# Linear attention's first chunk on Trainium2: reciprocals spread by quarter-array products, folded weights by halves, diagonal blocks set by GpSimd copies

## The chip, the cores and the metric

The kernel runs on one core of one Trainium2 chip, in one launch. The metric is the device time in microseconds; the profiled execution gives every instruction's start and duration. Five engines run side by side, each working through its own queue in order and waiting on semaphores: TensorE (PE; its weight loads are shown as PEld), VectorE (DVE), ScalarE (ACT), GpSimd (POOL) and SyncE (SP), which here issues the DMA transfers.

## The reference

Four layers act on x of 2048 rows by 576 columns in bf16: attention, MLP, attention, MLP, each added to x. The kernel calls them layers 0 to 3; the change touches layers 0 and 2.

```python
def _A_ref(x, wqkv, wo):                       # H = 32 heads of Dh = 18
    q, k, v = ...(x @ wqkv)...
    phi = lambda t: jnp.where(t > 0, t + 1, jnp.exp(t)) + 1e-6
    pq, pk = phi(q), phi(k)
    kv = jnp.einsum("bhsd,bhse->bhde", pk, v)
    z = jnp.einsum("bhsd->bhd", pk)
    num = jnp.einsum("bhqd,bhde->bhqe", pq, kv)
    den = jnp.einsum("bhqd,bhd->bhq", pq, z)[..., None] + 1e-6
    o = num / den
    return ...(o)... @ wo
def _B_ref(x, w1, b1, w2, b2):
    y = _layernorm(x, axis=-1)
    return gelu(y @ w1 + b1) @ w2 + b2
x = x + _A_ref(_layernorm(x), A_wqkv, A_wo)
x = x + _B_ref(_layernorm(x), B_w1, B_b1, B_w2, B_b2)   # and both once more
```

## The kernel before

The 2048 rows are 16 row blocks (t) of 128, in four chunks (c) of 512. The 32 heads are five groups (g): four of 7 heads (126 columns) and one of 4 heads (72 columns). The queries are held with their columns on the partitions, so a query tile pq[(g, c)] has 126 (or 72) partitions and 512 rows of x along it.

An attention layer (layer_A) first makes keys and query tiles for most of x. Its second part, where the change lies, runs once the sum over all keys is there:

- z (L789) and from it zsel, which sums a head's columns against z.
- den_stage(c), L820 to L828: 20 small TensorE products give the denominators of a chunk, 32 heads by 4 row blocks on 128 partitions; ScalarE takes the logarithm (L824) and the exponential of its negative (L827), which leaves the reciprocals in the single tile rden.
- quad_stage(c), L834: VectorE multiplies rden with a mask of four diagonal blocks, quad_mask, into a 128x512 tile quad_rden.
- scale_stage(g, c): one 512-wide TensorE product with head_bc (L847) spreads the reciprocals of a group over its 18 columns a head; ScalarE copies the bank (L851), VectorE multiplies the query tile (L852). With direct=True VectorE reads the bank itself.
- quarter_stage(c), L863, for later chunks: 16 products of 32 rows by 126 columns, 128 wide, for groups 0 to 3; each uses a quarter of TensorE's rows, takes rden as it is and needs no diagonal blocks. ScalarE copies four banks into the scratch tile turned (L867); quarter_scale multiplies (L873). Group 4 of these chunks still goes through scale_stage, and so through quad_rden.
- kv_groups (L693, then L699 and L704 with a mask) gives kvT; kv_wo(g) and kv_wo_half(g, half) fold the output weights into it: two 288-wide products a group, copied to kvwo. Groups 0 and 1 are folded earlier by halves (L711, L716), groups 2 to 4 here by kv_wo through a pair of banks (L799), copied by ScalarE (L806) or VectorE (L804).
- wo_stage(t), L883: ten products a row block, then the residual sum on VectorE (L598), the store of x, and for the first four row blocks the LayerNorm of the next layer. For these GpSimd takes the power (L428), one small product (L431), the normalised rows (L461) and a copy of their last 64 columns (L469).

TensorE's order is written out by hand: every product is chained to the one before (pe), so a product that waits holds everything behind it. The order of the other queues comes from a scheduler, steered by manual dependencies such as dve_after or "sums first".

PSUM has four single banks (ps_h, used in turn; a new use waits until the last reader is done) and two pairs, accA and accB (ps_acc). TensorE's order in the edited part is: a query product, den_stage(0), kv_groups, the second query product, folding of groups 2 and 3, three spreading products, folding of group 4, the fourth, the third query product, the fifth, den_stage(1), the last query product, row block 0. The four query products there (q_left) belong to chunk 3. In the loop over t, den_stage(2) and (3) come at t = 2 and t = 5, quarter_stage(1), (2), (3) at t = 1, 3, 7, and scale_stage(4, c) at t = 2, 4, 8.

Of the kernel before, what the change touches and what calls it, by code (L numbers as in the profile page):

```python
# [8 lines left out]
ALU = mybir.AluOpType  # L9
# [6 lines left out]
P = 128  # L16
# [18 lines left out]
def build(tc, A_x, A_wqkv, A_wo, B_w1, B_b1, B_w2, B_b2, out, dbg=None, n_layers=4):  # L35
    nc = tc.nc
    dbg = dbg or {}
    with ExitStack() as ctx:
# [23 lines left out]
        quad_mask = const.tile([P, 4, P], BF16, name="quad_mask")  # L62
# [15 lines left out]
        def cut(start, shape, fill, op, base, pattern, mult):  # L78
# [15 lines left out]
            cut(8, (4,), 0.0, ALU.is_ge, 0, [[-32, 4]], 1),  # L94
            cut(8, (4,), 0.0, ALU.is_ge, 31, [[32, 4]], -1),
# [163 lines left out]
        dve_last = dict(norm=None, sum=None, phi=None)  # L259
# [280 lines left out]
        def phi_from_psum(ps_ap, out_ap, rows, n, turned_cols=False, after=None, dve_after=None, exp_first=False,  # L540
                          tag=None):
# [11 lines left out]
            low = nc.vector.tensor_scalar(out=e[0:rows, 0:n], in0=e[0:rows, 0:n], scalar1=1.0, scalar2=1e-6,  # L553
                                          op0=ALU.min, op1=ALU.add)
            top = nc.vector.tensor_tensor(out=out_ap, in0=a[0:rows, 0:n], in1=e[0:rows, 0:n], op=ALU.max)
            if dve_after is not None:
                tc.add_manual_dep(top.ins, dve_after, NOSYNC, reason="denominators first")
            dve_last["phi"] = top.ins.name
            if tag is not None:
                named("e" + tag, exp), named("id" + tag, ident_pass), named("mi" + tag, low), named("ma" + tag, top)  # L560
# [47 lines left out]
        def layer_A(li, next_kind, pre_a1=None):  # L608
            pq = {}

            def q_proj(g, c, defer=False):
# [5 lines left out]
                pq[(g, c)] = first_pq if first_pq is not None and (g, c) == (0, 0) else \  # L617
                        blk.tile([P, D], BF16, name="pq", tag="blk")
                if g == 0:
                    if first_pq is None or c > 0:  # L620
                        (nc.gpsimd if li > 0 else nc.vector).memset(pq[(g, c)][96:P, 0:CA], 1.0)
# [64 lines left out]
            def kv_groups(groups):  # L686
# [12 lines left out]
                nc.vector.tensor_tensor(  # L699
# [3 lines left out]
                if 4 in groups:  # L703
                    nc.vector.tensor_tensor(  # L704
                        out=kvT[0:72, 4, 0:72].rearrange("p (h e) -> p h e", h=4),
                        in0=ps[0:72, 126 * n:126 * n + 72].rearrange("p (h e) -> p h e", h=4),
                        in1=maskz[0:72, 0:4, :], op=ALU.mult)
# [88 lines left out]
            def kv_wo(g):  # L796
                wp = ps_acc.tile([P, 2, 512], F32, name="kvwo_ps", tag=("accB", "accA")[g % 2])
                for half in range(2):
                    pe(nc.tensor.matmul(wp[0:GR[g], half, 0:HALF], lhsT=kvT[0:GR[g], g, 0:GR[g]],  # L799
                                     rhs=wo_sb[0:GR[g], g, half * HALF:(half + 1) * HALF], start=True, stop=True))  # L800
                kvwo[g] = blk.tile([P, D], BF16, name="kvwo", tag="blk")
                out = kvwo[g][0:GR[g], :].rearrange("p (h n) -> p h n", h=2)
                if g in (3, 4):
                    nc.vector.tensor_copy(out=out, in_=wp[0:GR[g], :, 0:HALF])  # L804
                else:
                    act_last["kvwo"] = nc.scalar.copy(out=out, in_=wp[0:GR[g], :, 0:HALF]).ins.name  # L806

            quad_rden = {}
            rden_of = {}
            rden_now = {}  # L810

            def den_stage(c, after=None, pair=None):
# [16 lines left out]
                rden_of[c] = rden  # L829
                rden_now["tile"] = rden  # L830

            def quad_stage(c, after=None):
                quad = blk.tile([P, D], BF16, name="quad_rden", tag="blk")
                spread_out = nc.vector.tensor_tensor(  # L834
                    out=quad[:, 0:CA].rearrange("p (j n) -> p j n", j=4), in0=quad_mask[:],
                    in1=rden_of.pop(c)[:].unsqueeze(1).to_broadcast([P, 4, P]), op=ALU.mult)
                if after is not None:
                    tc.add_manual_dep(spread_out.ins, after, NOSYNC, reason="sums first")
                quad_rden[c] = quad
                dve_last["quad"] = spread_out.ins.name  # L840

            def scale_stage(g, c, pair=None, direct=False):
# [4 lines left out]
                pe(nc.tensor.matmul(bp[:, 0:CA], lhsT=head_bc[:, g, :], rhs=quad_rden[c][:, 0:CA], start=True, stop=True))  # L847
                spread_rows = bp
                if not direct:
                    spread_rows = blk.tile([P, D], BF16, name="rden_bc", tag="blk")  # L850
                    act_last["copy"] = nc.scalar.copy(out=spread_rows[0:GR[g], 0:CA], in_=bp[0:GR[g], :]).ins.name  # L851
                mult = nc.vector.tensor_tensor(out=pq[(g, c)][0:GR[g], 0:CA], in0=pq[(g, c)][0:GR[g], 0:CA],  # L852
                                               in1=spread_rows[0:GR[g], 0:CA], op=ALU.mult)
                dve_last["mult"] = mult.ins.name

            def quarter_stage(c):

                rden = rden_now["tile"]
                banks = [ps_h.tile([P, 512], F32, name="rden_ps", tag="h") for _ in range(4)]
# [6 lines left out]
                for i in range(4):  # L866
                    act_last["copy"] = nc.scalar.copy(out=spread_rows[0:126, i, 0:4 * P], in_=banks[i][0:126, :]).ins.name  # L867

            def quarter_scale(c, groups, after):
                spread_rows = turned[:].rearrange("p a t c -> p (a t c)").rearrange("p (i w) -> p i w", i=4)  # L870
                for g in groups:
# [4 lines left out]
                    dve_last["mult"] = mult.ins.name  # L876
# [292 lines left out]
```

## Time and profile before

| | us |
|---|---|
| median of 3 runs (762.48 to 763.7) | 762.74 |
| profiled execution | 762.86 |
| its span in the profile | 761.1 |
| TensorE busy | 755.4 (99%) |
| ScalarE busy | 327.4 (43%) |
| VectorE busy | 271.2 (36%) |
| GpSimd busy | 119.1 (16%) |

The profiled execution is 1.76 us longer than its span. The granted TensorE clock is full in all slices. Layer 0's edited part runs from 70 to 104 us, layer 2's from 442 to 476 us.

In the timeline a row is: start, duration, engine, line, operation, output<-input, sizes and count, and in brackets the idle time ahead of it on its engine and what ended it. Rows with a count cover instructions that follow each other; TensorE's products are pipelined, so a product's row is longer than the time until the next one starts, and starts are what to compare.

### The profile page before, as it was taken

To read this page: it belongs to the slowest core of one execution; us is meant where nothing else is said; L and a number is where in the kernel's file an instruction comes from. 1 tells how busy PE (TensorE), PEld (TensorE's weight loads), DVE (VectorE), ACT (ScalarE), POOL (GpSimd) and SP (SyncE) were. 2 spreads that over 40 slices of the span, in tenths; PEclk is the share of its full clock that TensorE was granted. 3 is DMA by queue.
4 is the path that set the end of the run, shared out by engine and by line. 5 is a ranking of instruction groups with operands and counts; after the bars stand their busy time and mean duration, and the time that the engine had idled before them with its cause. 6 is when DMAs were issued, how large, how long until landed. Compare 5 with 4: busy or idle time off the path is not lost.

```text
span 761.1 us, 15693 instructions
## 1 busy us (share of the span) xinstructions
PE 755.4 (99%) x6539; PEld 489.0 (64%) x6539; DVE 271.2 (36%) x683; ACT 327.4 (43%) x731; POOL 119.1 (16%) x194
## 2 busy tenths in 40 slices
PE   8999999999999999999999999999999999999998
PEld 5777654774477457646777767447645754674476
DVE  8875962136023503401455678600230132000000
ACT  6884756205600650263056566560164036205600
POOL 4840341002000301200100005300020020001000
PEclk9999999999999999999999999999999999999999
DMA  8992573017302711320246007530240033011000
GB/s 255 267 309 51 169 269 83 16 58 196 82 31 84 185 53 47 108 69 16 73 122 202 1 32 244 193 83 16 76 104 29 16 125 83 9 32 55 2 10 23
DMA packets 80897, 73.82 MB, mean 97 GB/s; under 512 B 36730, under 2 KB 65466, under 8 KB 80826
## 3 DMA queue, kind: packets, MB, share of 16 engines
q1 hardware_dynamic: 80826, 72.82, 32.9%
q8 instruction: 51, 0.84, 0.5%
q14 instruction: 20, 0.16, 0.1%
HBM read 48.03 MB, written 24.77 MB: 96 GB/s over the span
## 4 chain that ended last, share of the span: by engine, by line
PE 94%; DMA 2%; DVE 2%; ACT 1%; issue 0%; SPq 0%; DVEq 0%; ACTq 0%
PE m_ps L1060 36%; PE h_ps L1002 20%; PE hp_ps L1002 16%; PE q_ps L614 6%; PE k_ps L644 5%; PE k_ps L669 4%; PE wo_ps L883 2%; PE m_half L1060 1%; PE k_tail L669 1%; DMA xo<-x_d 1%; DMA x_d<-xo 1%; PE tp L493 1%; ACT turned L867 1%; DMA x<-in_A_x_dram 0%; PE kv_ps L693 0%
## 5 line engine op out<-in xcount | busy, mean ns | idle before, releaser
L1060 PE MATMUL m_ps<-w_sb,hT 128*128 128x288 bf16 x2232 | 274.8, 286 | 0.0
L1060 PEld LDWEIGHTS <-hT 128*128 128x128 bf16 x2304 | 224.8, 98 | 59.8 <-issue 3.4
L1002 PEld LDWEIGHTS <-w_sb 64*128 64x128 bf16 x2304 | 124.5, 94 | 136.5 <-issue 1.9
L1002 PE MATMUL hp_ps<-yT,w_sb 64*128 64x512 bf16 x1152 | 178.0, 376 | 0.0
L1002 PE MATMUL h_ps<-yT,w_sb 64*128 64x512 bf16 x1152 | 148.0, 376 | 0.0
L1007 ACT COPY relay_sb<-relay_sb 128x1 f32<-128x1 f32 x144 | 28.6, 198 | 260.2 <-PE h_ps L1002 217.9
L998 ACT ACTIVATE hT<-h_ps,b1T 128x512 bf16<-128x512 f32 x144 | 91.2, 684 | 44.4 <-PE h_ps L1002 44.4
L428 POOL TENSOR_TENSOR ln_rstd<-ln_u,neg_half 128x1 f32<-128x1 f32 x61 | 35.4, 581 | 408.3 <-DVE ln_u L410 225.3
L998 ACT ACTIVATE hT<-hp_ps,b1T 128x512 bf16<-128x512 f32 x144 | 91.2, 693 | 0.0
L598 DVE TENSOR_TENSOR xbf<-m_ps,xo 128x576 bf16<-128x576 f32 x15 | 11.4, 758 | 212.9 <-PE m_ps L1060 212.9
L598 DVE TENSOR_TENSOR xo<-m_ps,xo 128x576 f32<-128x576 f32 x16 | 12.1, 757 | 176.5 <-PE m_ps L1060 176.5
L581 POOL TENSOR_TENSOR xo<-xo,b_bc 128x576 f32<-128x576 f32 x32 | 40.9, 1284 | 101.3 <-DMA xo<-x_d 62.7
L1002 PE MATMUL h_ps<-yT,w_tail 64*128 64x512 bf16 x144 | 54.1, 376 | 0.0
L1002 PE MATMUL hp_ps<-yT,w_tail 64*128 64x512 bf16 x144 | 54.1, 376 | 0.0
L614 PE MATMUL q_ps<-yT,wqkv_sb 128*126 128x512 bf16 (+1 forms) x200 | 49.5, 379 | 0.0
L644 PE MATMUL k_ps<-wqkv_sb,yT 128*128 128x288 bf16 x320 | 47.0, 286 | 0.3 <-ACT yT L495 0.3
L883 PE MATMUL wo_ps<-kvwo,pq 126*128 126x288 bf16 (+1 forms) x320 | 44.5, 286 | 0.2
L1002 PEld LDWEIGHTS <-w_tail 64*128 64x128 bf16 x288 | 27.1, 94 | 17.1
L644 PEld LDWEIGHTS <-yT 128*128 128x128 bf16 x320 | 30.9, 98 | 8.9 <-ACT yT L495 1.0
L883 PEld LDWEIGHTS <-pq 126*128 126x128 bf16 (+1 forms) x320 | 29.8, 97 | 10.3 <-DVE pq L873 0.7
L614 PEld LDWEIGHTS <-wqkv_sb 128*126 128x126 bf16 (+1 forms) x200 | 25.4, 131 | 11.8
L295 DVE STREAM_TRANSPOSE turned<-y_ring 128x576 bf16<-128x576 bf16 x40 | 30.3, 766 | 0.4
(141 smaller groups left out, 595.7 us busy)
## 6 DMA issues: line engine op xcount, KB each, us to landing
xo<-x_d SPq DMA_DIRECT2D x48, 288.0 KB
x_d<-xo SPq DMA_DIRECT2D x32, 288.0 KB
xl<-x_d SPq DMA_DIRECT2D x24, 288.0 KB
y_d<-turned SPq DMA_DIRECT2D x40, 144.0 KB
w_sb<-in_B_w_dram SPq DMA_DIRECT2D x6, 864.0 KB
yT<-y_d SPq DMA_DIRECT2D x10, 512.0 KB
w_sb<-in_B_w_dram SPq DMA_DIRECT2D x9, 512.0 KB
x_d<-xn SPq DMA_DIRECT2D x16, 288.0 KB
```

The source lines that it names most:

```text
L295: turn = nc.vector.transpose(out=turned[:, :, j, :], in_=y[:, 0:D])
L428: nc.gpsimd.tensor_tensor(out=rstd[:], in0=it["u"][:], in1=neg_half[:], op=ALU.pow)
L581: nc.gpsimd.tensor_tensor(out=xo[:], in0=xo[:], in1=b2_bc[:], op=ALU.add)
L598: total = nc.vector.tensor_tensor(out=xn[:, cols].rearrange("p (h n) -> p h n", h=2), in0=halves, in1=xo[:, cols].rearrange("p (h n) -> p ...
L614: pe(nc.tensor.matmul(qp[0:GR[g], :], lhsT=wqkv_sb[:, k, GO[g]:GO[g] + GR[g]], rhs=yT[:, k, c * CA:(c + 1) * CA], start=(k == 0), stop=(k ...
L644: pe(nc.tensor.matmul(kp[:, 0:HALF], lhsT=yT[:, k, t * P:(t + 1) * P], rhs=wqkv_sb[:, k, D + half * HALF: D + (half + 1) * HALF], start=(k ...
L669: pe(nc.tensor.matmul(dst, lhsT=lhsT, rhs=pk, start=(t == 0), stop=(t == NT - 1)))
L883: pe(nc.tensor.matmul(wp[:, half, 0:HALF], lhsT=pq[(g, c)][0:GR[g], j * P:(j + 1) * P], rhs=kvwo[g][0:GR[g], half * HALF:(half + 1) * HALF ...
L998: act_last["gelu"] = nc.scalar.activation(out=to, in_=ps, func=ACT.Gelu_apprx_tanh, bias=b1T[:, f:f + 1], scale=1.0).ins.name
L1002: mm = pe(nc.tensor.matmul(dst[n], lhsT=wt, rhs=mv, start=(seen[n] == 0), stop=(seen[n] == 8)))
L1007: relay = nc.scalar.copy(out=relay_sb[:, 1:2], in_=relay_sb[:, 0:1])
L1060: pe(nc.tensor.matmul(acc[half][:, 0:HALF], lhsT=hT[f][:, j * P:(j + 1) * P], rhs=w2_sb[:, f, half * HALF:(half + 1) * HALF], start=(f == ...
```

## The change

- The first chunk's groups 0 to 3 go through quarter_stage(0, pairs=True), whose four banks are the pairs accA and accB, and quarter_scale; group 4 goes through scale_stage with a ScalarE copy.
- quad_rden becomes one fixed tile, cleared once on VectorE where quad_mask was made; the mask's two select steps go. quad_stage sets its four diagonal blocks by four GpSimd copies of 32x128 from rden, right after each den_stage.
- Groups 2 to 4 are folded by kv_wo_half through single banks, all six copies on VectorE (by_dve); kv_wo goes.
- The query functions of two of the late products are split: ScalarE's part is issued early, VectorE's part (finish) behind the multiplies of the first chunk. The first query's exponential stands ahead of the logarithm on ScalarE, its second pass behind rden.
- TensorE's order becomes: query product, den_stage(0), kv_groups, quarter products, folding halves of groups 2 and 3, second query product, two halves of group 4, one spreading product for group 4, third query product, den_stage(1), the last query product, row block 0. Behind that it is as before. In the built program GpSimd's queue holds the copies of chunks 0 and 1 ahead of the first LayerNorm tile, those of chunk 2 behind it; those of chunk 3 follow at once in layer 0, and in layer 2 stand behind the second tile. SyncE's queue is the same.

```diff
-        quad_mask = const.tile([P, 4, P], BF16, name="quad_mask")
+        quad_rden = const.tile([P, 4 * P], BF16, name="quad_rden")
...
-                wide = nc.vector.tensor_copy(out=quad_mask[:], in_=small[:, 8:12].unsqueeze(2).to_broadcast([P, 4, P]))
+                wide = nc.vector.memset(quad_rden[:], 0.0)
...
-            def kv_wo_half(g, half):
+            def kv_wo_half(g, half, by_dve=False):
...
-                copy = nc.vector.tensor_copy if half else nc.scalar.copy
-                copy(out=kvwo[g][0:GR[g], half * HALF:(half + 1) * HALF], in_=wp[0:GR[g], 0:HALF])
+                copy = nc.vector.tensor_copy if half or by_dve else nc.scalar.copy
+                copy = copy(out=kvwo[g][0:GR[g], half * HALF:(half + 1) * HALF], in_=wp[0:GR[g], 0:HALF])
+                if by_dve:
+                    tc.add_manual_dep(copy.ins, dve_last["kvwo"], NOSYNC, reason="folded weights in order")
...
-            def quad_stage(c, after=None):
-                quad = blk.tile([P, D], BF16, name="quad_rden", tag="blk")
-                spread_out = nc.vector.tensor_tensor(
-                    out=quad[:, 0:CA].rearrange("p (j n) -> p j n", j=4), in0=quad_mask[:],
-                    in1=rden_of.pop(c)[:].unsqueeze(1).to_broadcast([P, 4, P]), op=ALU.mult)
...
+            def quad_stage():
+
+                for i in range(4):
+                    rows = slice(32 * i, 32 * (i + 1))
+                    nc.gpsimd.tensor_copy(out=quad_rden[rows, i * P:(i + 1) * P], in_=rden_now["tile"][rows, :])
...
-            def quarter_stage(c):
+            def quarter_stage(c, pairs=False, after=None):
 
                 rden = rden_now["tile"]
-                banks = [ps_h.tile([P, 512], F32, name="rden_ps", tag="h") for _ in range(4)]
+                if pairs:
+                    both = [ps_acc.tile([P, 2, 512], F32, name="rden_pair", tag=tag) for tag in ("accA", "accB")]
+                    banks = [both[i // 2][:, i % 2, :] for i in range(4)]
+                else:
+                    banks = [ps_h.tile([P, 512], F32, name="rden_ps", tag="h") for _ in range(4)]
...
-            phi = q_proj(*q_left.pop(0), defer=True)
-            den_stage(0)
-            quad_stage(0)
-            phi(after=act_last["rden"], dve_after=dve_last["quad"])
-            kv_groups((2, 3, 4))
-            late = [q_proj(*q_left.pop(0), defer=True)]
-            kv_wo(2)
-            kv_wo(3)
-            for g in range(3):
-                scale_stage(g, 0)
-            kv_wo(4)
-            scale_stage(3, 0, pair="accA")
-            late.append(q_proj(*q_left.pop(0), defer=True))
-            scale_stage(4, 0, direct=True)
+            first_query = q_proj(*q_left.pop(0), split=True)()
+            steps = act_last["phi_steps"]
+            den_stage(0, after=steps[0].name)
+            tc.add_manual_dep(steps[1], act_last["rden"], NOSYNC, reason="denominators first")
+            kv_groups((2, 3, 4))
+            quad_stage()
+            quarter_stage(0, pairs=True, after=steps[1].name)
+            dve_last["kvwo"] = dve_last["kv"]
+            for half in range(4):
+                kv_wo_half(2 + half // 2, half % 2, by_dve=True)
+            second_query = q_proj(*q_left.pop(0), split=True)(after=act_last["copy"])
+            for half in range(2):
+                kv_wo_half(4, half, by_dve=True)
+            quarter_scale(0, (0, 1, 2, 3), after=dve_last["kvwo"])
+            scale_stage(4, 0, pair="accA", act_after=act_last["phi"], dve_after=dve_last["mult"])
+            first_query(dve_after=dve_last["mult"])
+            second_query(dve_after=dve_last["phi"])
+            phi = q_proj(*q_left.pop(0), defer=True)
             den_stage(1, after=act_last["copy"], pair="accB")
-            quad_stage(1, after=dve_last["mult"])
-            for phi in late:
-                phi(after=act_last["rden"])
+            quad_stage()
+            phi(after=act_last["rden"])
...
                     den_stage(c + 2)
-                    if c > 0:
-                        quad_stage(c + 2, after=total)
-                if t == 3:
-                    quad_stage(2, after=total)
+                    quad_stage()
```

More of the change, by code (lines that the diff above doesn't have):

```diff
@@ L258, in build @@
         pool_last = dict(norm=None)
-        dve_last = dict(norm=None, sum=None, phi=None)
+        dve_last = dict(norm=None, sum=None, phi=None, kvwo=None, kv=None)
         landing = []
@@ L552, in phi_from_psum, with finish @@
             act_last["exp"], act_last["phi"] = exp.ins.name, ident_pass.ins.name
[L553 to L560, printed above, removed]
+            act_last["phi_steps"] = exp.ins, ident_pass.ins
+            def finish(dve_after=dve_after):
+                low = nc.vector.tensor_scalar(out=e[0:rows, 0:n], in0=e[0:rows, 0:n], scalar1=1.0, scalar2=1e-6,
+                                              op0=ALU.min, op1=ALU.add)
+                top = nc.vector.tensor_tensor(out=out_ap() if split else out_ap, in0=a[0:rows, 0:n], in1=e[0:rows, 0:n],
+                                              op=ALU.max)
+                if dve_after is not None:
+                    for step in (low, top):
+                        tc.add_manual_dep(step.ins, dve_after, NOSYNC, reason="first chunk first")
+                dve_last["phi"] = top.ins.name
+                if tag is not None:
+                    named("e" + tag, exp), named("id" + tag, ident_pass), named("mi" + tag, low), named("ma" + tag, top)
+            if split:
+                return finish
+            finish()
         xo_of = {}
@@ L616, in q_proj, with out_tile @@
                                      start=(k == 0), stop=(k == KD - 1)))
-                pq[(g, c)] = first_pq if first_pq is not None and (g, c) == (0, 0) else \
+                def out_tile():
+                    pq[(g, c)] = first_pq if first_pq is not None and (g, c) == (0, 0) else \
                         blk.tile([P, D], BF16, name="pq", tag="blk")
-                if g == 0:
-                    if first_pq is None or c > 0:
-                        (nc.gpsimd if li > 0 else nc.vector).memset(pq[(g, c)][96:P, 0:CA], 1.0)
+                    if g == 0:
+                        if first_pq is None or c > 0:
+                            (nc.gpsimd if li > 0 else nc.vector).memset(pq[(g, c)][96:P, 0:CA], 1.0)
+                    return pq[(g, c)][0:GR[g], 0:CA]
+                if split:
+                    return lambda after=None: phi_from_psum(qp[0:GR[g], :], out_tile, GR[g], CA, turned_cols=(li > 0),
+                                                            after=after, split=True)
+                out_tile()
                 phi = lambda after=None, dve_after=None, exp_first=False: phi_from_psum(qp[0:GR[g], :], pq[(g, c)][0:GR[g], 0:CA], GR[g], CA,
@@ L714, in kv_wo_half @@
                     kvwo[g] = blk.tile([P, D], BF16, name="kvwo", tag="blk")
-                copy = nc.vector.tensor_copy if half else nc.scalar.copy
-                copy(out=kvwo[g][0:GR[g], half * HALF:(half + 1) * HALF], in_=wp[0:GR[g], 0:HALF])
+                copy = nc.vector.tensor_copy if half or by_dve else nc.scalar.copy
+                copy = copy(out=kvwo[g][0:GR[g], half * HALF:(half + 1) * HALF], in_=wp[0:GR[g], 0:HALF])
+                if by_dve:
+                    tc.add_manual_dep(copy.ins, dve_last["kvwo"], NOSYNC, reason="folded weights in order")
+                    dve_last["kvwo"] = copy.ins.name
             if li == 0:
@@ L794, in layer_A @@
                                     in1=zp[0:72, 4:5].to_broadcast([72, H]), op=ALU.mult)
[L796 to L809, printed above, removed]
             rden_now = {}
@@ L828, in den_stage, with scale_stage @@
                                                         scale=-1.0).ins.name
-                rden_of[c] = rden
                 rden_now["tile"] = rden
-            def quad_stage(c, after=None):
-                quad = blk.tile([P, D], BF16, name="quad_rden", tag="blk")
-                spread_out = nc.vector.tensor_tensor(
-                    out=quad[:, 0:CA].rearrange("p (j n) -> p j n", j=4), in0=quad_mask[:],
-                    in1=rden_of.pop(c)[:].unsqueeze(1).to_broadcast([P, 4, P]), op=ALU.mult)
[L837 to L842, printed above, removed]
+            def quad_stage():
+                for i in range(4):
+                    rows = slice(32 * i, 32 * (i + 1))
+                    nc.gpsimd.tensor_copy(out=quad_rden[rows, i * P:(i + 1) * P], in_=rden_now["tile"][rows, :])
+            def scale_stage(g, c, pair=None, act_after=None, dve_after=None):
                 if pair:
@@ L846, in scale_stage @@
                     bp = ps_h.tile([P, 512], F32, name="rden_ps", tag="h")
[L847 to L851, printed above, removed]
+                pe(nc.tensor.matmul(bp[:, 0:CA], lhsT=head_bc[:, g, :], rhs=quad_rden[:], start=True, stop=True))
+                spread_rows = blk.tile([P, D], BF16, name="rden_bc", tag="blk")
+                copy = nc.scalar.copy(out=spread_rows[0:GR[g], 0:CA], in_=bp[0:GR[g], :])
+                act_last["copy"] = copy.ins.name
+                if act_after is not None:
+                    tc.add_manual_dep(copy.ins, act_after, NOSYNC, reason="queries' banks first")
                 mult = nc.vector.tensor_tensor(out=pq[(g, c)][0:GR[g], 0:CA], in0=pq[(g, c)][0:GR[g], 0:CA],
                                                in1=spread_rows[0:GR[g], 0:CA], op=ALU.mult)
+                if dve_after is not None:
+                    tc.add_manual_dep(mult.ins, dve_after, NOSYNC, reason="four groups first")
                 dve_last["mult"] = mult.ins.name
-            def quarter_stage(c):
+            def quarter_stage(c, pairs=False, after=None):
                 rden = rden_now["tile"]
-                banks = [ps_h.tile([P, 512], F32, name="rden_ps", tag="h") for _ in range(4)]
+                if pairs:
[3 more added lines that the diff above has]
+                    banks = [ps_h.tile([P, 512], F32, name="rden_ps", tag="h") for _ in range(4)]
                 for g in range(4):
@@ L866, in quarter_stage @@
                 for i in range(4):
-                    act_last["copy"] = nc.scalar.copy(out=spread_rows[0:126, i, 0:4 * P], in_=banks[i][0:126, :]).ins.name
+                    copy = nc.scalar.copy(out=spread_rows[0:126, i, 0:4 * P], in_=banks[i][0:126, :])
+                    if after is not None:
+                        tc.add_manual_dep(copy.ins, after, NOSYNC, reason="queries' banks first")
+                    act_last["copy"] = copy.ins.name
             def quarter_scale(c, groups, after):
@@ L875, in quarter_scale @@
                     tc.add_manual_dep(mult.ins, after, NOSYNC, reason="sums first")
-                    dve_last["mult"] = mult.ins.name
+                    after = dve_last["mult"] = mult.ins.name
             def wo_stage(t):
```

11 lines of the change are left out of this document (5 added, 6 removed).

## The prediction

> **What bounds the kernel now.** The page first: TensorE (PE) is busy nearly all the time and is 94% of the chain that ended last, so an edit counts as far as it moves TensorE's stream.
>
> ```profile
> PE 755.4 (99%) x6539; PEld 489.0 (64%) x6539; DVE 271.2 (36%) x683; ACT 327.4 (43%) x731; POOL 119.1 (16%) x194
> PE 94%; DMA 2%; DVE 2%; ACT 1%; issue 0%; SPq 0%; DVEq 0%; ACTq 0%
> ```
>
> Then the timeline of layer 0 from 70 us, the edited stage (layer 2 repeats it 372.64 us later within a few hundredths). Columns: start, duration, engine, line, operation, count, idle before.
>
> ```profile
> 72.47 1.27 PE L614 MATMUL q_ps<-yT,wqkv_sb 128*126 128x512 bf16 x5
> 72.80 0.41 DVE L699 TENSOR_TENSOR kvT<-kv_ps,maskz 126x252 bf16<-126x252 f32 x1
> 73.58 0.66 PE L799 MATMUL kvwo_ps<-wo_sb,kvT 126*126 126x288 bf16 x4
> 74.07 0.81 PE L847 MATMUL rden_ps<-quad_rden,head_bc 128*128 128x512 bf16 x3
> 78.18 2.63 PE L883 MATMUL wo_ps<-kvwo,pq 126*128 126x288 bf16 x20
> 80.74 0.45 PE L863 MATMUL rden_ps<-rden,head_bc 32*126 32x128 bf16 x16
> 81.12 1.40 PE L883 MATMUL wo_ps<-kvwo,pq 126*128 126x288 bf16 x10
> ```
>
> Read the starts: nearly every group begins where the one before has issued its last product, so the stage is dense. The 16 quarter-array products (L863) take 0.38 us till the next group; three 512-wide ones (L847) take 0.65, 0.215 each.
>
> Last, the same view from 83 us, with GpSimd (POOL).
>
> ```profile
> 83.17 0.15 DVE L413 TENSOR_SCALAR ln_u<-ln_mv 128x1 f32<-128x1 f32 x1
> 83.41 0.55 POOL L428 TENSOR_TENSOR ln_rstd<-ln_u,neg_half 128x1 f32<-128x1 f32 x1 [18.78 <-DVE ln_u L413]
> 84.79 1.89 PE L883 MATMUL wo_ps<-kvwo,pq 126*128 126x288 bf16 x10
> 84.85 1.39 POOL L461 TENSOR_SCALAR y_ring<-xn,ln_rstd,ln_nmr 128x576 bf16<-128x576 f32 x1
> 86.30 0.41 DVE L834 TENSOR_TENSOR quad_rden<-quad_mask,rden 128x512 bf16<-128x512 bf16 x1
> 86.30 0.50 POOL L469 COPY y_ring<-y_ring 128x64 bf16<-128x64 bf16 x1
> 86.76 0.10 PEld L847 LDWEIGHTS <-head_bc 128*128 128x128 bf16 x1 [0.40 <-DVE quad_rden L834]
> ```
>
> Here TensorE does stand: it needs the block-diagonal reciprocals of the third chunk at 86.76 and waits for VectorE's L834. In that stretch GpSimd works on a LayerNorm tile from 83.41 to 86.80. In the changed program the four copies that replace L834 stand behind that very tile in GpSimd's queue. This decides the forecast.
>
> **First chunk, layer 0 (then times two).** Removed: four 512-wide products, 4 x 0.215 = 0.86 us; and the 0.11 by which the fifth group's folding pair (74.72) is longer till 75.08 than two 0.125 products. Added: one quarter set, 0.38, plus 0.09 to enter it (a lone L847 at 76.37 takes 0.31 till the row-tiled products behind it, against 0.215 elsewhere). Net so far -0.50. Folding by halves keeps its six 288-wide products.
>
> Two waits come in. (1) With the query product gone from between, the first folding half follows the quarter set, ready at 72.47 + 0.09 + 0.38 = 72.94. It needs kvT. VectorE no longer does L834 ahead of it, so L699 starts when the kv products end, 72.67 instead of 72.80, ends 73.09, and 0.05 later (86.71 to 86.76 above) TensorE has it: wait 0.20. (2) The next query product takes the bank of the first folding half and waits for its copy, now on VectorE: product from 73.14, 0.29 long, copy 0.46 (L716's VectorE rows), so 73.98, where TensorE is ready at 73.14 + 4 x 0.12 = 73.63: wait 0.35. Together +0.55. The reciprocals come no later: ScalarE fits the first query's exponential (0.59, next start 0.47 later) between 71.39 and the logarithm at 71.86, which started at 71.85 before. Copies of the quarter set (ScalarE, 0.5 each from 73.0) end at 75.1, the pair's next use is at 75.3; the folding copies of group 4 (VectorE, 0.38 apart) end by 76.2, the five multiplies by 77.9, ahead of the first output product. Sum -0.50 + 0.55 = +0.05: the L883 at 78.18 moves to about 78.23. I bound this at -0.5 (no waits) and +0.3 (both half again as long) per layer.
>
> **VectorE up to the third chunk.** L834 of the second chunk (0.42 at 77.85) leaves the queue, so the two late query functions, the first two residual sums and the statistics move up: the last multiply ends 77.9, the minimum and maximum of the first query 78.67, which frees ScalarE's second phi_a buffer; the first sum starts 80.05 (80.15 before), the statistics 81.7 (82.02). So ln_u comes 0.33 earlier, and so do the multiplies of the second chunk, which cost TensorE 0.48 of the 0.73 us lost between 84.79 and 86.76. It is ready for the L847 product at about 86.17.
>
> **GpSimd.** The chain from L428 to the end of L469 took 3.39 us (83.41 to 86.80). It begins 0.33 earlier, and its last copy should take 0.24 (the row at 99.77, with no two-input VectorE work beside it) instead of 0.50, since the L834 that ran beside it is gone: end 86.80 - 0.33 - 0.26 = 86.21. Then four 32x128 copies, which no row shows. Nearest: 128x36 cast 0.22, 128x64 copy 0.24, so 0.86 ns an element and 0.295 us for 128; a following independent GpSimd instruction starts 0.02 to 0.05 before the end (L439's pairs), so 3 x 0.25 + 0.295 = 1.03. Bounds of the spacing: 0.14 (the mask steps L85 at 24.3, four elements wide) and 0.50 (the copy beside VectorE). I take 0.25, the uncontended copies being nearest: in that gap VectorE has only a PSUM sum. Ready for TensorE 86.21 + 1.03 + 0.05 = 87.29 against 86.76: **+0.53**. The waits of the first chunk are inside this, as GpSimd's end and not TensorE's now sets it.
>
> The copies elsewhere are hidden: the first chunk's (from 72.5) are needed at 75.3; the second's (from 77.8) at 82.37; the fourth's in layer 0 follow its reciprocals (89.47) and are needed at 93.19. In layer 2 they stand behind a second LayerNorm tile: its 3.8 us (459.44 to 463.26) begin after the third chunk's copies, about 459.8, and 1.0 for themselves makes 464.6, needed at 465.74 plus the shift; with copies of 0.50 it is 466.6 against 467.2, still covered. Reciprocals are overwritten by the next chunk only after the copies, but that exponential comes 1.5 us later or more.
>
> **Layer 2.** Same +0.53, but its tail has slack: TensorE stands 0.22 at 472.94 and 0.19 at 474.38 for residual rows, whose chain runs from the store at 462.55 (4.61 us) over the load at 467.17 (5.17) to the sum at 472.47. That store follows the sum of row block 5, held by VectorE till 461.42; the later products would end near 461.5. So the rows come 0.1 later and TensorE 0.53: 0.41 is absorbed, +0.12 left.
>
> **Sum.** 0.53 + 0.12 = +0.65. The profiled execution took 762.86 (761.1 span and 1.76 around it), 0.12 above the median of the runs, 762.74; on the median this gives 763.4. The masks' two select steps and the wide mask (now a clearing) lie under dense TensorE work at 20 to 60 us: nothing. A difference of 0.2%, 1.53 us, is about what a measurement tells from no change.
>
> **Rivals.**
> - *Copies overlap.* Spacing as in L85's tiny steps, 0.14: 3 x 0.14 + 0.295 = 0.72, so +0.2 in layer 0 and nothing left in layer 2: 762.9. For it: the copies touch separate rows and wait for nothing of each other. Against: a 128x512 L439 delays its follower by its full length. Chance 0.20. The Trainium skill, page "GPSIMD Engine Reference", section 2.1 (Instruction dispatch), says that each of GpSimd's cores serves 16 partitions of every instruction and goes on to the next when its own share is done. By that rule copies of four different sets of 32 rows run side by side; no row of this trace has such copies.
> - *Slower: the copies are dear.* With spacing p, the delay a layer is 86.21 + 4p + 0.05 - 86.76 = 4p - 0.50; two layers less 0.41 give 8p - 1.41, over 1.53 from p = 0.37 on. At 0.50 it is +2.6: 765.3. For it: L469 took 0.50 and even 1.09 at 462.17 beside VectorE's two-input work, L431 0.68 for one element; the multiplies of the third chunk (from about 87.1) can meet the last copy. Chance 0.31.
> - *Faster.* The first-chunk waits do not appear (-0.50 a layer) and the LayerNorm tile runs at its uncontended 0.82 instead of 1.39 and the copies overlap, so that GpSimd ends at 86.21 - 0.57 + 0.72 = 86.36 or before and the third-chunk wait goes too (-0.4 or more): about -1.8 in both layers, 760.9. Against: the multiplies run beside that tile in both programs. Chance 0.07.
> - *Forecast,* spacing 0.20 to 0.37: 0.42.
>
> **How the numbers follow.** Same: 0.42 + 0.20 = 0.62; slower 0.31; faster 0.07. The range takes in -0.9 (copies overlap, one layer's waits absent) to +2.9 (p near 0.5, first stage +0.3): 761.8 to 765.6. The forecast case alone: 762.9 to 764.3.
>
> **What would show it.** L847's load in the third chunk waiting for POOL quad_rden in both layers, with four POOL copies of about 0.3 right behind L469; L863 in the first chunk, x16, about 0.38 long; waits near 72.94 (for kvT) and 73.63 (for the first folding copy) of 0.2 and 0.35; first L883 within 0.3 of 78.18; ln_u about 0.3 earlier; the 472 to 475 waits in layer 2 smaller. Wrong if the first L883 moves by over 0.5, if the copies end before TensorE asks (86.2), or if the difference lies outside 70 to 104 and 442 to 476.

## The result and the profile after

| | before | after |
|---|---|---|
| median of 17 runs, us | 762.58 (762.33 to 763.7) | 764.38 (764.3 to 764.81) |
| profiled execution, us | 762.86 | 764.41 |
| its span, us | 761.1 | 762.6 |

The ratio is 1.0022 with a 95% interval of 1.0015 to 1.003: 1.80 us slower. The forecast was 763.4. The two profiled executions differ by 1.55, because the one of before lies 0.28 above its kernel's median and the one of after 0.03.

The page of after: TensorE has lost 1.2 us of work (755.4 to 754.2) and the span is longer all the same, and GpSimd has entered the chain that ended last.

```profile
PE 754.2 (99%) x6563; PEld 489.5 (64%) x6563; DVE 269.0 (35%) x683; ACT 328.1 (43%) x731; POOL 127.4 (17%) x224
PE 95%; DVE 2%; ACT 1%; POOL 1%; issue 1%; DMA 0%; ACTq 0%; POOLq 0%; DVEq 0%
```

Apart from the masks at the start of the program, the edited stages begin behind the first z product (L789, now L808), so they are compared from its start: 69.75 us before and 69.83 after in layer 0, 442.39 and 443.53 in layer 2. On the axis of layer 0 the rows of after thus stand 0.08 late.

The timeline of after, layer 0, first chunk (start, duration, engine, line, operation, tiles, count, idle before):

```profile
72.64 0.45 PE L870 MATMUL rden_pair<-rden,head_bc 32*126 32x128 bf16 x16
72.75 0.42 DVE L714 TENSOR_TENSOR kvT<-kv_ps,maskz 126x252 bf16<-126x252 f32 x1 [1.61 <-PE kv_ps L708]
...
73.22 0.70 PE L727 MATMUL kvwo_half<-wo_sb,kvT 126*126 126x288 bf16 x4
73.60 1.55 DVE L732 CAST kvwo<-kvwo_half 126x288 bf16<-126x288 f32 x4 [0.29 <-PE kvwo_half L727]
74.11 1.24 PE L621 MATMUL q_ps<-yT,wqkv_sb 128*126 128x512 bf16 x5 [0.18 <-DVE kvwo L732]
```

Both waits that the prediction put into this stage are here: the first folding half starts 0.05 after kvT's end (73.17), the second query product behind VectorE's first folding copy.

The same view at the third chunk:

```profile
82.96 0.15 DVE L411 TENSOR_SCALAR ln_u<-ln_mv 128x1 f32<-128x1 f32 x1
...
84.64 1.39 POOL L459 TENSOR_SCALAR y_ring<-xn,ln_rstd,ln_nmr 128x576 bf16<-128x576 f32 x1
...
86.09 0.24 POOL L467 COPY y_ring<-y_ring 128x64 bf16<-128x64 bf16 x1
...
86.26 1.33 POOL L840 COPY quad_rden<-rden 32x128 bf16<-32x128 bf16 x4
...
87.65 0.38 PE L847 MATMUL rden_ps<-quad_rden,head_bc 128*128 128x512 bf16 x1 [1.19 <-POOL quad_rden L840]
```

The wait has changed its owner, from VectorE's L834 to GpSimd's L840, and it is longer. The copies follow the LayerNorm tile (L459, L467) at once and take 1.33 us.

Third, at the end of layer 0, ScalarE and TensorE. First before:

```profile
90.44 0.69 ACT L498 COPY yT<-tp 128x640 bf16<-128x640 bf16 x1 [0.31 <-PE tp L493]
91.03 0.78 ACT L383 ACTIVATE ln_dump<-xn,ln_mv 128x576 bf16<-128x576 f32 x1
91.56 0.31 PEld L863 LDWEIGHTS <-head_bc 32*126 32x126 bf16 x16 [0.24 <-issue]
```

and after:

```profile
91.25 0.78 ACT L381 ACTIVATE ln_dump<-xn,ln_mv 128x576 bf16<-128x576 f32 x1
...
92.03 0.67 ACT L496 COPY yT<-tp 128x640 bf16<-128x640 bf16 x1
...
92.44 0.70 PE L870 MATMUL rden_ps<-rden,head_bc 32*126 32x128 bf16 x16
92.75 0.25 PEld L870 LDWEIGHTS <-head_bc 32*126 32x126 bf16 x12 [0.18 <-issue]
```

ScalarE's copy of the turned rows and its statistics pass have changed places. The last quarter set loads the weights of its first four products, stops, and loads on at 92.75, 0.05 after that copy's end at 92.70: the set takes 0.64 us until the next group instead of 0.38. The prediction had no term for this.

Summed from the first z product, in us, after less before:

| | layer 0 | layer 2 |
|---|---|---|
| first output product | +0.07 | +0.06 |
| third chunk's spreading product (L847) | +0.81 | +0.76 |
| last quarter set (L870) | +0.26 | +0.10 |
| from there to the MLP's first product | -0.02 | -0.51 |
| MLP's first product | +1.05 | +0.35 |

The second row holds the first, and the last row is the sum of the three above it. Of layer 2's -0.51, 0.49 is in two groups of output products that had lost it to waits before. The two stages together thus make +1.40; with the 0.08 ahead of the first z product this is 1.48 of the 1.55 by which the two profiled executions differ, so the difference lies in the two edited stretches. The medians differ by 0.25 more. In which rows that lies is not shown, since each kernel has one profile.

### The profile page after: what moved, and what is told of

The parts are those of the page before. It is cut to its first block, busy times and chain, and to the rows that moved or that the text cites. A ratio compares the mean times of both kernels' runs of the same rounds, so it can differ in the third digit from the quotient of the medians.

```text
span 762.6 us, 15782 instructions
## 1 busy us (share of the span) xinstructions
PE 754.2 (99%) x6563; PEld 489.5 (64%) x6563; DVE 269.0 (35%) x683; ACT 328.1 (43%) x731; POOL 127.4 (17%) x224
## 4 chain that ended last, share of the span: by engine, by line
PE 95%; DVE 2%; ACT 1%; POOL 1%; issue 1%; DMA 0%; ACTq 0%; POOLq 0%; DVEq 0%
PE m_ps L1070 36%; PE h_ps L1012 20%; PE hp_ps L1012 16%; PE q_ps L621 6%; PE k_ps L659 5%; PE k_ps L684 4%; PE wo_ps L893 4%; PE m_half L1070 1%; PE k_tail L684 1%; PE tp L491 1%; PE kv_ps L708 0%; DMA x<-in_A_x_dram 0%; ACT turned L874 0%; PE kvwo_half L727 0%; POOL quad_rden L840 0%
## 5 line engine op out<-in xcount | busy, mean ns | idle before, releaser
L545 ACT ACTIVATE phi_e<-q_ps 126x512 bf16<-126x512 f32 (+1 forms) x40 | 23.9, 597 | 15.8 <-PE q_ps L621 15.8
```

## Experiments

All were timed beside the kernel before on the same chip, whose medians there were 762.59 to 762.69. "Behind z" is the time from the start of the first z product, for layers 0 and 2. Line numbers shift by a few where a kernel has another length.

**Which part costs.** `vector_blocks` is the changed kernel with the diagonal blocks made by VectorE's mask product again, so the first-chunk part alone.

```diff
-            def quad_stage():
-                for i in range(4):
-                    rows = slice(32 * i, 32 * (i + 1))
-                    nc.gpsimd.tensor_copy(out=quad_rden[rows, i * P:(i + 1) * P], in_=rden_now["tile"][rows, :])
+            def quad_stage(c, after=None):
+                ...  # L834 of the kernel before, with its mask and its places
```

> The changed kernel with the diagonal blocks made by VectorE's masked product again, for chunks 2 and 3 behind the residual sums as in the kernel before; the rest of the change (quarter products, folding by halves, split queries) stays. So this is the first-chunk part of the change alone. Queue theory: the third-chunk wait falls from 1.35 to some 0.3 us a layer, first output product within 0.3 us of the changed kernel's; total 762.4 (762.0 to 762.9). Rival one: the first-chunk waits are all there, so 764.2 or more.

`pool_blocks_alone` is the kernel before with that one function exchanged the other way round, GpSimd's copies in place of L834.

> The kernel before with the diagonal blocks set by GpSimd copies into one tile, and nothing else of the change. Queue theory: the LayerNorm tile ends at 86.5 (its last copy 0.24 instead of 0.50), four copies 1.33, so the third-chunk product starts 1.1 to 1.2 us later than before in each layer, less 0.5 in layer 2's tail; the quarter products of chunk 3 lose 0.26 in layer 0 as ScalarE's copy of the turned rows goes behind a statistics pass here too. Total 764.6 (764.2 to 765.2). Rival one: 762.6, as before. Rival two: between 763 and 764.4 without any TensorE wait at that product.

Measured: 762.0 (ratio 0.9992, 0.9983 to 1.0) and 765.0 (1.0031, 1.0019 to 1.0043). The first-chunk part brings -0.59, the copies cost +2.41, and the sum, +1.82, is what both together cost (+1.80). The third chunk in the timeline of `vector_blocks`, then of `pool_blocks_alone`:

```profile
86.36 0.41 DVE L843 TENSOR_TENSOR quad_rden<-quad_mask,rden 128x512 bf16<-128x512 bf16 x1
...
86.83 0.10 PEld L856 LDWEIGHTS <-head_bc 128*128 128x128 bf16 x1 [0.39 <-DVE quad_rden L843]
```

```profile
86.54 0.24 POOL L467 COPY y_ring<-y_ring 128x64 bf16<-128x64 bf16 x1
...
86.71 1.32 POOL L831 COPY quad_rden<-rden 32x128 bf16<-32x128 bf16 x4
...
88.09 0.38 PE L838 MATMUL rden_ps<-quad_rden,head_bc 128*128 128x512 bf16 x1 [1.17 <-POOL quad_rden L831]
```

Behind z the product stands at 16.79 and 16.68 in the first, at 18.16 and 18.01 in the second (17.01 and 16.92 before). The first output product is at 8.50 in the first as in the changed kernel, so what the first-chunk part brings does not come from there. VectorE is ahead in its queue, so that the mask product for which TensorE waits starts at 16.31 instead of 16.55 behind z in layer 0, and layer 2's tail is 0.4 shorter. The 762.0 lies at the lower edge of what was expected.

**Is it the copies' length?** `copies_twice` makes the third chunk's four copies twice.

```diff
-                    quad_stage()
+                    quad_stage(2 if c == 0 else 1)   # the loop over the four copies, twice
```

> The changed kernel with the four GpSimd copies of chunk 2 made twice over (the second set writes the same values). Queue theory: the third-chunk product starts 1.3 us later in each layer, and no slack is left in layer 2's tail: 767.0 (766.6 to 767.4). If four copies on separate rows ran side by side, or the queue were not on the path: under 765.5. Rival one: 764.4.

Measured: 767.52 (1.0076, 1.006 to 1.0091), 3.14 above the changed kernel and just above the expected range. The product stands at 19.35 and 19.26 behind z, 1.53 and 1.58 later, which together make 3.11.

```profile
86.20 2.87 POOL L840 COPY quad_rden<-rden 32x128 bf16<-32x128 bf16 x8
...
89.12 0.58 PE L847 MATMUL rden_ps<-quad_rden,head_bc 128*128 128x512 bf16 x1 [2.72 <-POOL quad_rden L840]
...
89.50 2.60 PE L893 MATMUL wo_ps<-kvwo,pq 126*128 126x288 bf16 x10
```

Eight copies end to end, 0.36 each on average; what the second set adds goes through to TensorE. The last two rows show a second price, which is not in the median. The profiled execution took 771.5. In it TensorE's granted clock fell to 0.50 from 88.31 us on, inside the wait of 2.72, and came back at 95.14; the output products there start 0.24 apart instead of 0.12. In layer 2 it fell again, from 467.19 to 470.60. Of the six executions this one and one of 769.32 had a mean clock below full (0.993 and 0.998); the other four, at full clock, took 767.43 to 767.55. Behind the 1.2 us wait of the changed kernel the clock stayed full.

**Or when they are wanted?** `late_use` moves the third chunk's spreading product one row block later.

```diff
-                    if j == (2 if c == 0 else 0):
+                    if j == (2 if c == 0 else 1 if c == 1 else 0):
                         scale_stage(4, c + 1)
```

> The changed kernel with one product moved: the 512-wide product that spreads group 4 of chunk 2 is issued at row block 5 instead of 4; all GpSimd copies stay as they are. Queue theory (the loss is TensorE standing behind a product that waits for four copies queued after a LayerNorm tile on GpSimd): of the 1.35 us wait in layer 0 about 0.1 is left, since ten output products (1.32 us) now run in it; layer 2 gains less, as its tail waits for residual rows again. Total 762.4, 1.7 to 2.2 below the changed kernel. Rival one (the loss is the two new waits of the first chunk, 0.27 and 0.48 us a layer): no change, 764.4. Rival two (the copies slow other engines at SBUF): no change, 764.4.

Measured: 761.95 (0.9991, 0.9982 to 1.0), 2.43 below the changed kernel, more than the 1.7 to 2.2 expected. The copies are as they were, and of the wait little is left: the product starts 0.10 (layer 0) and 0.05 (layer 2) later behind its predecessor than in `before_late_use` below, where it starts 0.13 behind it.

```profile
86.21 1.32 POOL L840 COPY quad_rden<-rden 32x128 bf16<-32x128 bf16 x4
...
87.59 0.38 PE L847 MATMUL rden_ps<-quad_rden,head_bc 128*128 128x512 bf16 x1
```

**Or where they stand in the queue?** `copies_first` leaves the product where it is and puts the copies ahead of the LayerNorm tile, by one dependency.

```diff
+                            if it["kind"] == "B" and it["t"] == 0:
+                                tc.add_manual_dep(norm.ins, pool_last["quad"], NOSYNC, reason="blocks first")
```

> The changed kernel, with the third chunk's four GpSimd copies put ahead of the first LayerNorm tile's normalisation (L459) and its tail copy; the same instructions otherwise. Theory, place in GpSimd's queue: the copies start when rden is there and the small product L429 is done, 14.7 us behind the first z product, and end between 16.1 (0.345 apart) and 16.6 (0.5 apart, as beside VectorE's two-input work), so that the spreading product comes at 16.3 to 16.7 instead of 17.82: 1.1 to 1.5 us less in layer 0, the same less about 0.5 of the tail in layer 2. Expected 762.2 us (761.8 to 762.6). The LayerNorm tile then ends about 1.4 later, near 17.9, and is wanted by TensorE's transposes at about 19.9. Rival, the copies as such are too slow for that moment wherever they stand: the product stays near 17.5 and the time above 763.7. Second rival: the later LayerNorm tile holds the transposes, and the time comes back to 764.

Measured: 762.44 (0.9996, 0.9987 to 1.0006), 1.94 below the changed kernel; the product stands at 16.66 and 16.67.

```profile
84.46 1.68 POOL L842 COPY quad_rden<-rden 32x128 bf16<-32x128 bf16 x4
...
86.24 0.82 POOL L459 TENSOR_SCALAR y_ring<-xn,ln_rstd,ln_nmr 128x576 bf16<-128x576 f32 x1
...
86.46 0.38 PE L850 MATMUL rden_ps<-quad_rden,head_bc 128*128 128x512 bf16 x1
```

Here the copies meet VectorE's multiplies and are longer (1.68), and still the product does not wait for them. The LayerNorm tile, now behind the multiplies, takes 0.82 instead of 1.39. So the same four instructions cost 1.94 us less by their place alone. Against `vector_blocks` (762.0) 0.44 is left. The last quarter set takes 0.64 and 0.48 here as in the changed kernel, which is the next matter.

**The exchanged ScalarE steps.** `copy_order` is the changed kernel with the copy of the turned rows put back ahead of the statistics pass.

```diff
+                            if it["kind"] == "B" and it["t"] == 0:
+                                tc.add_manual_dep(self.square.ins, turned_tile.ins.name, NOSYNC, reason="turned rows first")
```

> The changed kernel, with ScalarE's copy of the first MLP row block's turned rows put ahead of the Square pass of the next LayerNorm statistics, as it stood before the change. Theory: the last quarter set of layer 0 took 0.638 us instead of 0.379 because its third bank waits for that copy, in layer 2 0.48; with the order back both take about 0.38, layer 0 is 0.26 us shorter, and of layer 2's 0.10 some is taken up by its tail. Expected 764.0 us, 0.3 below the changed kernel. Rival: the late GpSimd copies alone set the end of the attention layer, and what that set loses is made up before the MLP starts: then 764.4, and the start of the MLP stays 34.28 us behind the first z product.

Measured: 763.94 (1.0016, 1.0007 to 1.0025), 0.44 below the changed kernel. The MLP starts 34.02 and 33.86 behind z, 0.26 and 0.11 earlier, and the last quarter set is whole again:

```profile
91.19 0.69 ACT L496 COPY yT<-tp 128x640 bf16<-128x640 bf16 x1
91.78 0.78 ACT L381 ACTIVATE ln_dump<-xn,ln_mv 128x576 bf16<-128x576 f32 x1
...
92.32 0.45 PE L872 MATMUL rden_ps<-rden,head_bc 32*126 32x128 bf16 x16
```

The exchange is no answer to a late stage. It stands in all five kernels that have the copies and not this dependency, `copies_first` among them, where the product is early; in `vector_blocks` and `before_late_use`, which have the mask product, the order is as before. It came with the copies when the program was built; why the scheduler chose it was not tried.

`late_use_order` has both edits.

> The order of the run before and the third chunk's spreading product one row block later, both. Theory, costs that add: 761.95 us with the later product alone, less about 0.25: 761.7. Rival: with the later product the scheduler has the copy in time anyway (the last quarter set started 21.36 us behind the first z product in that run), so that nothing is left to gain: 761.95.

Measured: 761.69 (0.9983, 0.9975 to 0.9992), 0.26 below `late_use`; layer 0's MLP starts 32.79 behind z instead of 33.05, layer 2's at 32.73 in both. So the wait was there with the later product too, and the edit takes it away in layer 0 (0.65 to 0.38 for the set). In layer 2 the set takes 0.50 with either order, so something else holds it there; what that is was not tried.

**How much of that belongs to the change?** `before_late_use` is the kernel before with the later product.

> The kernel before, with the third chunk's spreading product one row block later. This tells how much of the gain of the later product has nothing to do with the change: it takes away the wait for VectorE's L834 (0.40 us idle on the weight load, at least 0.25 of it on TensorE's stream) in both layers, some of it given back by the tail of layer 2. Expected 762.2 us (762.0 to 762.4). Then the changed kernel with the later product, 761.95, owes at most 0.3 to the change itself. Rival: VectorE's product was in nobody's way, and the time stays 762.6.

Measured: 762.21 (0.9992, 0.9983 to 1.0002). The place of the product thus brings 0.40 without the change; with the wait all but gone in both, the change is worth 0.26 (761.95 against 762.21), about the size of the runs' own scatter.

**A better first stage.** `second_query_early` is `late_use_order` with TensorE's first stage in another order.

```diff
-            for half in range(4):
-                kv_wo_half(2 + half // 2, half % 2, by_dve=True)
-            second_query = q_proj(*q_left.pop(0), split=True)(after=act_last["copy"])
-            for half in range(2):
-                kv_wo_half(4, half, by_dve=True)
+            for half in range(2):
+                kv_wo_half(2, half, by_dve=True)
+            second_query = q_proj(*q_left.pop(0), split=True)(after=act_last["copy"])
+            for half in range(2):
+                kv_wo_half(3, half, by_dve=True)
...
             scale_stage(4, 0, pair="accA", act_after=act_last["phi"], dve_after=dve_last["mult"])
+            phi = q_proj(*q_left.pop(0), defer=True)
+            for half in range(2):
+                kv_wo_half(4, half)
             first_query(dve_after=dve_last["mult"])
             second_query(dve_after=dve_last["phi"])
-            phi = q_proj(*q_left.pop(0), defer=True)
```

> The order of late_use_order, with the first stage arranged anew so that no product asks for a bank whose copy has just begun: folding halves of group 2, second query product, halves of group 3, spreading product of group 4, third query product, halves of group 4 (their copies one on ScalarE, one on VectorE). Theory: the second of the two first-chunk waits, 0.35 us a layer, goes, the wait for kvT stays (0.2 to 0.27); two layers less what the tail takes up: 761.2 us (760.8 to 761.6). Rival: the multiplies of the first chunk or the later third query product's copy take the wait's place, and the first output product stays 8.50 us behind the first z product: 761.7.

Measured: 761.06 (0.998, 0.9972 to 0.9989): 1.55 below the kernel before, 0.63 below `late_use_order`.

```profile
73.19 0.46 PE L729 MATMUL kvwo_half<-wo_sb,kvT 126*126 126x288 bf16 x2
73.48 1.25 PE L623 MATMUL q_ps<-yT,wqkv_sb 128*126 128x512 bf16 x5
...
74.56 0.41 PE L729 MATMUL kvwo_half<-wo_sb,kvT 126*126 126x288 bf16 x2
```

The query product follows two folding halves without a wait, and the first output product stands at 8.16 behind z in both layers, 0.34 earlier: the price that the prediction gave this wait (0.35).

`second_query_vector` has the same order, with VectorE's mask product instead of the copies.

> The arrangement of second_query_early, with the diagonal blocks made by VectorE's product with the mask again instead of GpSimd's copies, in all chunks. It tells whether the copies bring anything once their wait is gone. Theory, both are hidden then: 761.1 us (760.9 to 761.3), and the third chunk's product waits for neither. Rival, VectorE's four products of 0.41 us a layer hold its multiplies up, and so the output products: 761.4 or more. Second rival, the copies slow VectorE or the LayerNorm tile: 760.8 or less.

Measured: 761.07 (0.9979, 0.9971 to 0.9988). With the wait down to 0.10 and 0.05, copies and mask product come to the same time: the GpSimd part of the change brings nothing here, its first-chunk part, in the new order, does.

## Why the prediction was right, and where its sizes were off

| step | predicted | measured (layer 0; layer 2) |
|---|---|---|
| first folding half, behind kvT | 73.14 | 73.14 (73.22 - 0.08) |
| second query product, behind VectorE's copy | 73.98 | 74.03 |
| first output product, a layer | +0.05 | +0.07; +0.06 |
| ln_u | -0.33 | -0.28; -0.29 |
| TensorE ready for the third chunk's product | 86.17 | 86.22 (last output product at 86.18, 0.12 for it, less 0.08) |
| LayerNorm tile's last copy | 0.24 long, ends 86.21 | 0.24, 86.25 |
| four copies | 1.03 | 1.33; 1.28 |
| third chunk's product | +0.53 | +0.81; +0.76 |
| last quarter set | 0 | +0.26; +0.10 |
| layer 2's tail | -0.41 | -0.49 |
| sum | +0.65 | +1.80 in the medians |

The mechanism was the predicted one: copies queued behind the LayerNorm tile, TensorE waiting for them in both layers, the first stage giving back in two waits what its fewer products save. `copies_twice`, `late_use` and `copies_first` show it from three sides (longer copies, later need, earlier place).

**The mis-sized term is the copies' spacing.** One copy lasts 0.286 to 0.295, as worked out from the rows of before (0.295). The spacing was taken as 0.25, from pairs in which a follower starts before its predecessor's end; the trace has each copy start 0.04 to 0.06 after the end of the one before, 0.345 apart in layer 0. That is 3 x 0.095 = 0.29 too little in layer 0. With 0.345 the prediction's own formula, 8p - 1.41, gives +1.35. That is 0.10 too much, because it counts the last copy as a spacing (0.345) and not as a length (0.295). Two smaller slips do no harm: 3 x 0.25 + 0.295 is 1.045, not 1.03, and the 73.98 for the second query product holds 0.09 more than the terms named for it.

**The missing term is ScalarE's order**, 0.26 + 0.10, which `copy_order` shows by undoing it. With it the sum is 1.71, against 1.80 in the medians, but that is closer than the account deserves. The terms as measured, 0.81 + 0.76 + 0.26 + 0.10 - 0.53, make 1.40: the third chunk's product is later by less than the formula says (by 0.19 in both layers together), and what is given back behind it, 0.53, is 0.12 more than the 0.41 of the formula. The prediction worked through GpSimd's and VectorE's queues and took ScalarE's order behind the third chunk as given; the step that failed is "the copies elsewhere are hidden", which priced the last chunk's copies and not what the copies change in the order of the other queues.

**Layer 2's tail** was nearly right in size. Its sums waited for residual rows before and wait for TensorE after; the fourth-last sum of each kernel, before and then after:

```profile
472.47 0.76 DVE L598 TENSOR_TENSOR xo<-wo_ps,xo 128x576 f32<-128x576 f32 x1 [1.29 <-DMA xo<-x_d]
```

```profile
473.68 0.76 DVE L605 TENSOR_TENSOR xo<-wo_ps,xo 128x576 f32<-128x576 f32 x1 [0.53 <-PE wo_ps L893]
```

But the reason given, products later than the rows, is not the whole of it: in `vector_blocks` and `before_late_use` the last spreading product is 0.24 and 0.26 earlier, and the tail behind it is 0.4 shorter too. There SyncE issues the load of the rows for this sum 23.43 and 24.39 behind z instead of 24.78. In the changed kernel it is issued at 24.30, 0.48 earlier, where the prediction had it 0.1 later. So the size was right in part by luck. What in SyncE's queue lets the load go earlier was not tried.

**The rivals.** Overlapping copies (0.20) did not happen: they run strictly one after another, in all chunks and kernels. By the rule of the Trainium skill, page "GPSIMD Engine Reference", section 2.1 (Instruction dispatch), each core goes on to the next instruction when its own share is done, so copies for different sets of 32 rows would run side by side. The traces here do not agree: every copy starts 0.04 to 0.06 after the end of the one before, and in `copies_twice` TensorE is released only behind the eighth. Dear copies (0.31, from a spacing of 0.37): the spacing stayed below, at 0.345, but with ScalarE's wait on top the time passed the bound of 1.53 us that this case was meant for. By its time the result belongs to this rival, by its spacing to the forecast. Faster (0.07): its condition, that the waits of the first chunk do not appear, failed as predicted; but `second_query_early` takes away one of them by order alone, and comes to the 760.9 of that rival within 0.2.

## What to carry to other kernels

An instruction that is moved to an idle engine takes its place in that engine's queue: price what stands ahead of it there, and then try its place before its length. Here four copies behind a LayerNorm tile cost 1.94 us more than the same four ahead of it, and 2.43 more than with their reader one row block later. When instructions move to another engine, compare the built order on all engines, since a scheduler can exchange two steps on a third one (here 0.36 us on ScalarE's account), and the price of that is in no step of the change itself.

## What was not expected of the hardware

- Four independent GpSimd copies of 32x128 bf16, each for other rows, took 0.29 us each and started 0.32 to 0.35 apart where no two-input VectorE instruction ran beside them. The number of rows hardly shows: a 128x64 copy, four times the rows and half the columns, took 0.24. What makes the gap of about 0.05 between them was not tried.
- Beside VectorE's two-input multiplies the copies took 0.39 to 0.49 (`copies_first`) and the multiplies lost as well, 1.51 instead of 1.42 for four and 0.50 instead of 0.42 for the fifth. The LayerNorm tile's 128x576 pass took 1.39 beside them and 0.82 behind them. The Trainium skill, page "SBUF — State Buffer", section "Who interferes with whom", says that a VectorE instruction with two inputs in SBUF contends with a GpSimd instruction that reads SBUF, and that such contention is an exclusive lock. The trace agrees: in both layers each of the first three copies ends 0.22 to 0.23 after the start of VectorE's next instruction, as if it had waited for the one beside it, and the fourth, beside a sum that reads PSUM, took 0.29. How much of a lengthened row is waiting the trace does not tell.
- In one execution of `copies_twice` TensorE's granted clock fell to 0.50 in one wait of 2.72 us and just behind the other, for 6.8 and 3.4 us; four of the six executions were at full clock. What decides between the two is not shown.
